# When an attention unit's output is normalised: the first unit earlier than the others

## The chip, the cores and the metric

The kernel runs on one core of a Trainium2 chip. The metric is the device time of one execution in microseconds, and the median of a few runs stands for a kernel. The core has five engines that work side by side, each through its own instructions in order: TensorE (PE in the profile, its weight loads PEld), VectorE (DVE), ScalarE (ACT), GpSimd (POOL) and SyncE (SP), which here issues nearly all DMA transfers.

## The reference

Four batches of eight-head attention over 576 positions with head dimension 64, whose scores carry a bias made by a tiny network from the distance of two positions; then a feed-forward layer with a rational activation over the 2304 tokens.

```
scores = q k^T / sqrt(64) + bias            # bias: relu(x w1 + b1) w2 per head, x from |i - j| and i
attn   = exp(scores - max) / (sum + 1e-9)
x      = attn v, heads side by side          # 2304 x 512
h      = x w_in                              # 2304 x 2048
g      = (a0 + a1 h + a2 h^2 + a3 h^3) / (1 + |b0||h| + |b1|h^2 + 1e-6)
out    = g w_out                             # 2304 x 512
```

## The kernel before

The program has three stages. The first makes the bias tables. The second, from about 45 to 270 us of the span, is attention; the third is the feed-forward layer, with each product as three float32r products of high and low halves.

Attention runs in *units*: unit u is one pair of heads of one batch, 16 in all (four pairs by four batches). A unit's 576 rows are cut into *steps* of 128 rows (the last 64 rows of two units share a step), 72 in all, and a *round* takes two steps. Round r forms the score products of steps 2r and 2r+1 (line 340), then, a round behind, transposes the probabilities of the two steps before (line 416), then multiplies transposed probabilities by V (line 485). DVE adds the bias and takes the row minimum of the negated scores (line 356), ACT takes the exponential (line 372) and copies the transposes out of PSUM (line 431). Each round DVE copies two products with V out of PSUM into the unit's tile `xs` (line 494). In the gaps of the rounds the layer's weights are split: POOL's copy `wm` (line 176), DVE's line 180, POOL's subtraction into `wil`/`wol` (line 187).

The sums of the exponentials are collected per unit; when a unit's last step is through, DVE adds 1e-9 and takes reciprocals, PE transposes them, DVE copies them to `rt`, and SP writes them to DRAM (`rs`, lines 455 and 460). `load_rb` (line 388) reads them back, broadcast over partitions, into `rb`. `e_norm` (line 400) multiplies `xs` by `rb` in place, on POOL for 14 of the 16 units, and puts a store of `xs` to DRAM (`xd`, line 402) on a list that the same round's end runs.

`done_to(k)` decides when: it is called at each round's end for the two steps that are complete; for unit u a step count `e` marks where the sums are ready (then `load_rb`), and a later count, the subject of the change, puts `e_norm` on the list `norms`. `rnd` takes at most one from this list in a round, into one of POOL's two places ("pool" ahead of DVE's score work, "pool2" after its first half) if the weight split has left that place empty. One round in three has both places taken.

Tiles come from pools that set when a buffer can be written again. `xs` has four buffers (`bufs=4`, line 490), so unit 4 writes into the buffer of unit 0, and its first write waits until unit 0's store has read it. `rb` has two, so unit 2's broadcast waits for unit 0's multiplication. SP issues in order; a transfer behind one that waits is not issued.

Of the kernel before, what the change touches and what calls it, by code (L numbers as in the profile page):

```python
# [37 lines left out]
def tile_attn_moe(  # L38
# [193 lines left out]
    with tc.manual_schedule():  # L232
# [3 lines left out]
        with ExitStack() as actx:  # L236
# [148 lines left out]
            def load_rb(u):  # L385
                t = rb[u] = npool.tile([P, S], F32, tag="rb", name=f"rb{u}")
                for j in range(2):
                    nc.sync.dma_start(  # L388
                        out=t[64 * j:64 * j + 64],
                        in_=rsum[u // 2][u % 2, j:j + 1, :].to_broadcast([64, S]),  # L390
                    )

            def e_norm(u):
                x = xs.pop(u)
                p, b = units[u]
                eng = V if u in (NX, NU - 1) else G
                f = rb.pop(u)

                def part(a, z):
                    op = eng.tensor_tensor(out=x[:, a:z], in0=x[:, a:z], in1=f[:, a:z], op=ALU.mult)  # L400
                    if z == S:
                        stores.append(lambda: nc.sync.dma_start(out=xd[b][:, p, :], in_=x))
                    return op

                return [lambda: part(0, S)]
# [95 lines left out]
            NS = len(steps)  # L501
            NU = len(units)
# [30 lines left out]
            def done_to(k):  # L533
                for u in range(NU - 1):
                    e = 2 * full[u]
                    if k == (e if u < NX else e - 2):
                        load_rb(u)
                    if u == NX:
                        if k == NS - 8:
                            x12.append(xs[u])  # L540
                            late.extend(e_norm(u))
                    elif k == (NS if u == NU - 2 else min(e + 4, NS - 3)):
                        norms.extend(e_norm(u))

            def run(todo):
# [43 lines left out]
            def rnd(r):  # L589
# [52 lines left out]
                if put:  # L642
                    put()
                run(stores)
                done_to(i - 2)
                done_to(i - 1)
                for x in plan["last"] + list(hi[1:]):
                    x()
# [11 lines left out]
            def finish():  # L660
                run(puts)
                mm1(0, 1)
                ZZ = (5, 7)
                main, ends, _, copy = e_tp(NS - 2, (2, 3), ZZ)
                weave(*(main[r] + ends[r] for r in range(2)))
                copy(1, 2)
                copy(0, 1)
                put_tails(NS - 2, 1, ZZ, ())
                recip(NS - 1)
                run(norms)  # L670
                run(stores)
                us = ended(NS - 1)
                main, ends, adds, copy = e_tp(NS - 1, (4, 6), ZZ, us)
                weave(*(main[r] + ends[r] + adds[r] for r in range(2)))
                copy(1, 2)
                copy(0, 1)
                put = [e_pv(NS - 3, 3), e_pv(NS - 2, 2)]
                put.pop(0)()
                put_tails(NS - 1, 1, ZZ, us)
                mm1(0, 0)  # L680
                put.pop(0)()
                put = e_pv(NS - 1, 6)
                done_to(NS)
                run(norms)
                run(stores)
                load_rb(NU - 1)
                load_x(1, 1, KD - 1, KD)
                put()

            with ExitStack() as bctx:  # L690
# [62 lines left out]
                for y, n in enumerate(order):  # L753
# [19 lines left out]
                    e = rpool.tile([P, EW], F32, tag="e", name=f"e{n}")  # L773
# [9 lines left out]
                    g, k = divmod(n, 8)  # L783
# [310 lines left out]
```

## Time and profile before

| | |
|---|---|
| median of 3 runs | 668.06 us (667.06 to 668.68) |
| profiled execution, own time | 667.56 us |
| its span, first to last instruction | 665.8 us |
| TensorE busy | 654.1 us, 98% of the span |
| VectorE busy | 561.6 us, 84% |
| ScalarE busy | 470.6 us, 71% |
| GpSimd busy | 153.5 us, 23% |
| mean granted TensorE clock | 0.995 |

Busy times are summed over an engine's instructions in the one profiled execution. Times on a row are microseconds from the span's start, and an idle time in brackets is what the engine waited before the instruction, with the event that ended it. Line numbers are those of the kernel.

### The profile page before, as it was taken

The page shows a single profiled execution, that of the slowest core. Times are in us where ns is not written, and L with a number is a line of the kernel's source. Part 1 is how long each engine was busy: PE and PEld are TensorE (multiplying, and loading weights), DVE is VectorE, ACT ScalarE, POOL GpSimd, SP SyncE. Part 2 cuts the span into 40 slices and gives each one's busy share as a digit, 9 for nine tenths or more (in the row PEclk, how much of TensorE's full clock was granted, in tenths as well). Part 3 has the DMA queues.
Part 4 walks back from the last instruction along what each step waited for, and adds up shares of the span by engine and source line. Part 5 has one row for each costly group of instructions (what it writes and reads, how often), then busy time and mean ns, then how long its engine had stood idle before and what let it go on. Part 6 is the DMA issues. An engine that isn't in the chain of part 4 may idle for free.

```text
span 665.8 us, 16141 instructions
## 1 busy us (share of the span) xinstructions
PE 654.1 (98%) x6276; PEld 550.0 (83%) x6276; DVE 561.6 (84%) x1102; ACT 470.6 (71%) x757; POOL 153.5 (23%) x108
## 2 busy tenths in 40 slices
PE   9999996999999999999999999999999999999997
PEld 6667885888888888988888888889988888888996
DVE  7997985888889996699998989979769779687776
ACT  7978996899999998677657466666655655455551
POOL 1000222334343340122122121222221221212211
PEclk9999998999999999999999999999999999999999
DMA  6898687688978974342744516768531301302031
GB/s 229 300 320 277 236 272 244 207 271 255 300 236 276 303 235 145 122 160 80 243 153 146 194 56 218 238 220 285 178 111 48 127 0 64 110 28 99 1 112 47
DMA packets 69901, 118.98 MB, mean 179 GB/s; under 512 B 9024, under 2 KB 30912, under 8 KB 69824
## 3 DMA queue, kind: packets, MB, share of 16 engines
q1 hardware_dynamic: 69680, 117.78, 53.6%
q8 instruction: 49, 0.80, 0.5%
q14 instruction: 28, 0.23, 0.1%
q10 hardware_dynamic: 144, 0.16, 0.1%
HBM read 79.17 MB, written 35.61 MB: 172 GB/s over the span
## 4 chain that ended last, share of the span: by engine, by line
PE 95%; ACT 2%; issue 1%; SPq 1%; DMA 1%; POOL 0%; DVE 0%; DVEq 0%; POOLq 0%
PE ps L313 30%; PE ps L922 30%; PE ps L485 12%; PE ps L340 11%; PE ps L769 6%; PE ps L416 6%; ACT p L372 1%; PE ps L720 1%; ACT pt L431 1%; DMA xd<-xs 1%; SPq L259 0%; POOL xs L400 0%; SPq L388 0%; DVE pre L943 0%; SPq L455 0%
## 5 line engine op out<-in xcount | busy, mean ns | idle before, releaser
L892 POOL TENSOR_TENSOR gl<-m,r 128x1024 fp32r<-128x1024 f32 (+1 forms) x39 | 85.6, 2194 | 299.5 <-DVE m L885 262.4
L843 ACT ACTIVATE w<-ps,babs 128x1024 f32<-128x1024 f32 (+1 forms) x40 | 41.2, 1031 | 107.8 <-PE ps L313 104.1
L372 ACT ACTIVATE p<-s,m 128x576 f32<-128x576 f32 x144 | 110.1, 781 | 0.6 <-DVE m L356 0.6
L356 DVE CUSTOM_DVE_ANT_0 s<-ps,bias 128x576 f32<-128x576 f32 (+1 forms) x144 | 95.2, 682 | 7.6 <-PE ps L340 3.3
L340 PE MATMUL ps<-qk 64*128 64x288 f32 (+1 forms) x640 | 82.8, 421 | 6.1 <-DVE xs L494 6.1
L431 ACT COPY pt<-ps 128x512 f32<-128x512 f32 (+1 forms) x109 | 71.8, 732 | 18.2 <-PE ps L416 18.2
L922 PE MATMUL ps<-wol,gh 128*128 128x512 f32 x216 | 84.2, 390 | 0.0
L922 PE MATMUL ps<-woh,gh 128*128 128x512 f32 x216 | 84.2, 390 | 0.0
L485 PE MATMUL ps<-pt,v 128*64 128x128 f32 (+1 forms) x1280 | 78.6, 266 | 0.8 <-ACT pt L431 0.5
L855 DVE SCALAR_TENSOR_TENSOR u<-w,babs,ps 128x1024 f32<-128x1024 f32 (+1 forms) x40 | 46.9, 1172 | 38.1 <-ACT t L844 38.0
L340 PEld LDWEIGHTS ps<-qk 64*128 64x128 f32 (+1 forms) x640 | 51.5, 177 | 26.0 <-DVE xs L494 7.5
L485 PEld LDWEIGHTS ps<-pt,v 128*64 128x64 f32 x1280 | 65.5, 137 | 5.7 <-ACT pt L431 1.6
L313 PE MATMUL ps<-xb,wih 128*128 128x512 f32 (+1 forms) x240 | 68.8, 367 | 0.0
L850 ACT ACTIVATE u<-u 128x1024 f32<-128x1024 f32 (+1 forms) x40 | 39.1, 977 | 40.2 <-DVE u L855 40.0
L416 PEld LDWEIGHTS ps<-ident,p 64*128 64x128 f32 x1296 | 51.1, 141 | 6.4 <-DVE m L356 0.6
L871 DVE SCALAR_TENSOR_TENSOR gh<-t,cst,r 128x1024 fp32r<-128x1024 f32 (+1 forms) x40 | 47.0, 1174 | 9.3 <-ACT r L852 6.9
L922 PE MATMUL ps<-woh,gl 128*128 128x512 f32 x216 | 53.8, 389 | 0.0
L416 PE MATMUL ps<-ident,p 64*128 64x64 f32 x1296 | 51.9, 228 | 0.1
L878 DVE SCALAR_TENSOR_TENSOR m<-u,qc,gh 128x1024 f32<-128x1024 f32 (+1 forms) x40 | 47.1, 1178 | 4.0
L313 PEld LDWEIGHTS ps<-xb,wih 128*128 128x128 f32 x240 | 44.5, 188 | 6.1
L885 DVE SCALAR_TENSOR_TENSOR m<-t,cst,m 128x1024 f32<-128x1024 f32 (+1 forms) x40 | 47.1, 1179 | 1.4
L864 DVE SCALAR_TENSOR_TENSOR t<-t,cst,ps 128x1024 f32<-128x1024 f32 (+1 forms) x40 | 47.0, 1175 | 1.4
(84 smaller groups left out, 1342.7 us busy)
## 6 DMA issues: line engine op xcount, KB each, us to landing
tab<-e SPq DMA_DIRECT2D x36, 295.5 KB
qk<-in_qkt_dram SPq DMA_DIRECT2D x16, 576.0 KB
wx<-in_w_in_dram SPq DMA_DIRECT2D x16, 512.0 KB
wx<-in_w_out_dram SPq DMA_DIRECT2D x16, 512.0 KB
v<-in_vp_dram SPq DMA_DIRECT2D x16, 320.0 KB
ws<-wh SPq DMA_DIRECT2D x20, 256.0 KB
ws<-wl SPq DMA_DIRECT2D x20, 256.0 KB
bias<-tab SPq DMA_DIRECT2D x16, 288.0 KB
```

Source lines behind the costliest of these rows:

```text
L313: on(T.matmul(hps[s][:, j, :w_], w[:, k, sl], x[:, k, :w_], start=(k == 0 and z == 0), stop=(k == KD - 1 and z == 2),), b + j)
L340: on(T.matmul(W[o, b, :SH], q[r, x], k[r, a * SH:(a + 1) * SH], start=True, stop=True), b)
L356: op = on(V.tensor_tensor_reduce(out=t3[:, a], in0=W[:, b:b + 2][:, a, :SH], in1=b3[:, a], scale=-0.125, scalar=least, op0=ALU.add, op1=AL ...
L372: A.activation(out=prob[i][:, z * S:z * S + S], in_=t, func=AF.Exp, bias=m, scale=-1.0, accum_out=sums[u % 4][:, k:k + 1],)
L416: on(T.transpose(W[:, b, o:o + 64], src[x, :], ident[x, x]), b)
L431: on(A.copy(out=t.rearrange("p x (r s) -> p r x s", r=2)[:, a:z], in_=W[:, to[a]:to[a] + z - a].rearrange("p r (x s) -> p r x s", s=64),), ...
L485: on(T.matmul(ps[y, o], vt[n][:, kc, y], w_, start=(kc == 0), stop=(kc == 4)), b, mem=(f"pt{i % 3}", f"tl{i // 2 % 2}"))
L864: on(V.scalar_tensor_tensor(out=rt[s, "t"], in0=rt[s, "t"], scalar=abs_[:, 1:2], in1=hp(s), op0=ALU.add, op1=ALU.mult,), *hb(s), mem="t")
L878: V.scalar_tensor_tensor(out=m, in0=rt[s, "u"], scalar=qc, in1=rt[s, "gh"].bitcast(F32), op0=ALU.add, op1=ALU.mult,)
L885: V.scalar_tensor_tensor(out=m, in0=rt[s, "t"], scalar=abs_[:, 0:1], in1=m, op0=ALU.add, op1=ALU.subtract)
L892: eng.tensor_tensor(out=lo, in0=rt[s, "m"], in1=rt[s, "r0"], op=ALU.mult)
L922: on(T.matmul(po[n, c], l[:, j, c * P:(c + 1) * P], r[fp][:, j, :], start=(first and x is a), stop=(last and x is z),), OB[c])
```

## The change

One number becomes an expression. For unit 0 the count that puts `e_norm` on the list is `e + 2`, for all others it stays `e + 4`.

```diff
@@ -539,7 +539,7 @@
                         if k == NS - 8:
                             x12.append(xs[u])
                             late.extend(e_norm(u))
-                    elif k == (NS if u == NU - 2 else min(e + 4, NS - 3)):
+                    elif k == (NS if u == NU - 2 else min(e + (4 if u else 2), NS - 3)):
                         norms.extend(e_norm(u))
```

For unit 0 `e` is 10. With `e + 4` the item goes on the list at the end of round 8; round 9 has no place, and round 10 takes it. With `e + 2` it goes on the list at the end of round 7, and round 8 has a place free. Unit 1's item, on the list from the end of round 9 in both kernels, finds round 10 free now, where before it went into round 11.

On POOL, in the rounds 7 to 11, the order before is this (a name's first number is the unit for `xs` and `rb`, the weight block for the others):

```order
L176 COPY wm1_0_1579<-wx1_0_1097 128x1024
L187 TENSOR_TENSOR wil0_897<-wm1_0_1579,wh1_0_1567 128x4x128
L176 COPY wm1_1_1816<-wx1_1_1099 128x1024
L187 TENSOR_TENSOR wol0_899<-wm1_1_1816,wh1_1_1692 128x512
L176 COPY wm2_0_1929<-wx2_0_1435 128x1024
L400 TENSOR_TENSOR xs0_990<-xs0_990,rb0_1554 128x576
L400 TENSOR_TENSOR xs1_1184<-xs1_1184,rb1_1677 128x576
L187 TENSOR_TENSOR wil1_901<-wm2_0_1929,wh2_0_1917 128x4x128
```

And in the changed kernel, on POOL in the same rounds:

```order
L176 COPY wm1_0_1579<-wx1_0_1097 128x1024
L400 TENSOR_TENSOR xs0_990<-xs0_990,rb0_1554 128x576
L187 TENSOR_TENSOR wil0_897<-wm1_0_1579,wh1_0_1567 128x4x128
L176 COPY wm1_1_1818<-wx1_1_1099 128x1024
L187 TENSOR_TENSOR wol0_899<-wm1_1_1818,wh1_1_1692 128x512
L176 COPY wm2_0_1931<-wx2_0_1435 128x1024
L400 TENSOR_TENSOR xs1_1184<-xs1_1184,rb1_1677 128x576
L187 TENSOR_TENSOR wil1_901<-wm2_0_1931,wh2_0_1919 128x4x128
```

Unit 0's multiplication has moved ahead of four weight instructions; unit 1's keeps its place in the sequence, but is tied to DVE's work of round 10, no longer of round 11.

On SP, from the end of round 8 to the end of round 10, the order before has unit 0's store of `xs` last:

```order
L460 DMA rs1_1765<-rt2_1764 2x2x64
L139 DMA wx3_0_1798<-in_w_in_dram 128x2048
L195 DMA woh0_898<-wh1_1_1692 128x512
L270 DMA v5_1801<-in_vp_dram 128x640
L264 DMA qk6_1803<-in_qkt_dram 128x1152
L388 DMA rb2_1905<-rs1_1765 64x576 x2
L139 DMA wx3_1_1908<-in_w_out_dram 128x2048
L259 DMA bias2_1910<-tab0_66 128x576
L259 DMA bias2_1910<-tab0_66 128x512
L259 DMA bias2_1910<-tab0_66 128x64
L455 DMA rs1_1765<-rt3_1990 2x4x128
L402 DMA xd0_71<-xs0_990 128x576
```

The changed kernel's SP has it in this place:

```order
L460 DMA rs1_1766<-rt2_1765 2x2x64
L402 DMA xd0_71<-xs0_990 128x576
L139 DMA wx3_0_1800<-in_w_in_dram 128x2048
L195 DMA woh0_898<-wh1_1_1692 128x512
L270 DMA v5_1803<-in_vp_dram 128x640
L264 DMA qk6_1805<-in_qkt_dram 128x1152
L388 DMA rb2_1907<-rs1_1766 64x576 x2
```

The store moves ahead of eleven issues, two weight loads (`wx`), the broadcast of unit 2 (`rb2`) and three bias loads among them.

Each of SP's issues also waits for one of eight DMA counters, DMAHW0 to DMAHW7, which the issues use in turn: an issue waits until the one eight places ahead has landed. For the broadcast of unit 0 this part of SP's order, the same in both kernels, is with its waits:

```order
L388 DMA rb0_1554<-rs0_1400 64x576 [waits DMAHW6_49]
L388 DMA rb0_1554<-rs0_1400 64x576 [waits DMAHW7_49]
L139 DMA wx2_1_1557<-in_w_out_dram 128x2048 [waits DMAHW0_49,Pool_49]
L259 DMA bias1_910<-tab3_69 128x576 [waits DMAHW1_49]
L259 DMA bias1_910<-tab3_69 128x512 [waits DMAHW2_49]
L259 DMA bias1_910<-tab3_69 128x64 [waits DMAHW3_49]
L264 DMA qk5_1562<-in_qkt_dram 128x1152 [waits DMAHW4_49,PE_49]
L388 DMA rb1_1677<-rs0_1400 64x576 [waits DMAHW5_49]
L388 DMA rb1_1677<-rs0_1400 64x576 [waits DMAHW6_49]
L195 DMA wih0_896<-wh1_0_1567 128x4x128 [waits DMAHW7_49,DVE_49]
```

Nothing moves here; the last row's issue waits for the second half of `rb0`, eight issues ahead of it.

## Rows read from the trace of the kernel before

**Rows 1.** The page, busy time of each engine.

```profile
PE 654.1 (98%) x6276; PEld 550.0 (83%) x6276; DVE 561.6 (84%) x1102; ACT 470.6 (71%) x757; POOL 153.5 (23%) x108
```

**Rows 2.** Chain of waits in order of time, 95 to 125 us: start, us, what.

```profile
104.75 1.42 POOL xs L400
...
106.19 0.47 SPq L388
...
111.01 3.60 DMA xd<-xs
...
115.08 2.29 PE ps L340 x8
```

**Rows 3.** Timeline of DVE: start, us, instruction, idle before it and releaser.

```profile
114.73 0.29 DVE L494 COPY xs<-ps 128x128 f32<-128x128 f32 x1 [6.99 <-DMA xd<-xs]
```

**Rows 4.** Timeline of PE, score products of round 11 and the next round's.

```profile
107.76 1.20 PE L340 MATMUL ps<-qk 64*64 64x288 f32 x16
115.08 2.29 PE L340 MATMUL ps<-qk 64*128 64x288 f32 x8 [6.12 <-DVE xs L494]
...
121.76 1.48 PE L340 MATMUL ps<-qk 64*128 64x288 f32 x10
```

**Rows 5.** Timeline of PE, first score products of rounds 6 and 7.

```profile
78.63 2.37 PE L340 MATMUL ps<-qk 64*64 64x288 f32 x24
...
84.51 1.73 PE L340 MATMUL ps<-qk 64*128 64x288 f32 x12
```

**Rows 6.** The same, first score products of rounds 15 and 16.

```profile
139.23 2.37 PE L340 MATMUL ps<-qk 64*64 64x288 f32 x24
...
145.11 2.21 PE L340 MATMUL ps<-qk 64*128 64x288 f32 x16
```

**Rows 7.** Engines by stretch: length, busy per engine (x instructions), PEclk, DMA share, GB/s.

```profile
98.00:100.00 2.00, 2.00 (x46) 1.74 (x44) 2.00 (x6) 1.22 (x5) 0.44 (x1) 1.00 0.11 27
108.00:115.00 7.00, 0.96 (x16) 0.31 (x8) 0.27 (x2) 1.80 (x6) 0.00 (x0) 0.85 0.95 291
115.00:121.00 6.00, 5.92 (x72) 5.14 (x74) 4.53 (x16) 3.46 (x6) 2.70 (x2) 0.61 0.51 147
121.00:660.00 539.00, 538.77 (x4320) 461.27 (x4317) 459.93 (x789) 370.01 (x560) 137.34 (x81) 1.00 0.49 160
```

**Rows 8.** Timeline of POOL, rounds 7 to 11.

```profile
85.44 1.04 POOL L176 COPY wm<-wx 128x1024 uint16<-128x1024 uint16 x1 [2.08 <-issue]
93.77 1.28 POOL L187 TENSOR_TENSOR wil<-wm,wh 128x512 fp32r<-128x512 f32 x1 [7.29 <-DVE wm L180]
96.81 1.04 POOL L176 COPY wm<-wx 128x1024 uint16<-128x1024 uint16 x1 [1.76 <-issue]
...
115.44 1.42 POOL L400 TENSOR_TENSOR xs<-xs,rb 128x576 f32<-128x576 f32 x1 [9.28 <-DVE wk L155]
```

**Rows 9.** Timeline of DVE, weight work of rounds 8, 9 and 11.

```profile
90.83 0.42 DVE L155 TENSOR_SCALAR wk<-wx 128x512 uint32<-128x512 uint32 x1
...
93.00 0.69 DVE L180 SCALAR_TENSOR_TENSOR wm<-wm,wh 128x512 uint32<-128x512 uint32 x1
...
98.79 0.69 DVE L180 SCALAR_TENSOR_TENSOR wm<-wm,wh 128x512 uint32<-128x512 uint32 x1
...
114.94 0.42 DVE L155 TENSOR_SCALAR wk<-wx 128x512 uint32<-128x512 uint32 x1
```

**Rows 10.** Timeline of SP's DMA issues, rounds 7 to 9.

```profile
84.64 1.13 SPq L388 DMA_DIRECT2D rb<-rs  x2
...
91.11 0.66 SPq L195 DMA_DIRECT2D wih<-wh  x1
...
98.60 0.26 SPq L460 DMA_DIRECT2D rs<-rt  x1
100.12 0.34 SPq L139 DMA_DIRECT2D wx<-in_w_in_dram  x1
...
101.18 0.54 SPq L270 DMA_DIRECT2D v<-in_vp_dram  x1
```

**Rows 11.** SP's issue and POOL's wait of one late unit.

```profile
252.12 1.11 SPq L388 DMA_DIRECT2D rb<-rs  x2
```

**Rows 12.** POOL's timeline for the same unit.

```profile
256.82 1.42 POOL L400 TENSOR_TENSOR xs<-xs,rb 128x576 f32<-128x576 f32 x1 [7.79 <-DMA rb<-rs]
```

## The prediction

> **What bounds the kernel now.** The page's busy times come first: TensorE is at work for 654.1 of 665.8 us [rows 1], so a change elsewhere counts only where TensorE stands still. Next, the chain of waits shows that the attention stage has one large hole. The chain leaves PE at about 101 us, runs through POOL's multiplication of unit 0, SP's queue and the store of `xs`, and comes back to PE at 115.08 [rows 2]. The timelines tell the same from both sides. DVE stood 6.99 us before its first copy into unit 4's `xs`, until the store of unit 0 had landed, since both units use one buffer [rows 3]; and PE stood 6.12 us in the middle of round 11's score products behind that copy [rows 4]. The stretches show what followed: the granted clock falls while PE stands (0.85 as the mean of 108 to 115 us), and from 115 to 121 us, with PE back at work, the mean is still 0.61, so that part of this stretch runs at 1.2 and not 2.4 GHz [rows 7]. From 121 to 660 us PE is busy for 538.77 of 539.00 us at clock 1.00 [rows 7]: nothing behind the hole would take back time gained there by already waiting for something else.
>
> **What the hole costs.** Not the 6.12 us alone, since the slow clock behind it belongs to it. I take whole rounds. Round 11 runs from 107.76 to round 12's first product at 121.76, 14.00 us [rows 4]. It has 24 score products, as every round with a shared 64-row step. Round 6, of the same shape, takes 84.51 - 78.63 = 5.88 us [rows 5], and round 15 takes 145.11 - 139.23 = 5.88 us [rows 6]. So the hole costs 14.00 - 5.88 = 8.12 us: 6.12 of standing still and 2.00 of slow clock. As a check, a mean of 0.61 over six microseconds is 0.39 x 6 = 2.3 us less of full clock, near 2.00.
>
> **The change part by part.** No instruction is added or removed, so busy times stay. Three things move.
>
> *Unit 0's multiplication*, one POOL instruction of 1.42 us [rows 8], goes from round 10 into round 8, ahead of the weight subtraction. It is tied to DVE's `wk` of that round, which ends at 90.83 + 0.42 = 91.25. In round 11 the same tie took 115.44 - (114.94 + 0.42) = 0.08 us [rows 8, 9], so it can start at 91.33 and end at 92.75. POOL has nothing to do between the end of a copy at 86.48 and 93.77 [rows 8], so the subtraction behind it is not moved: cost nothing, hidden in POOL's 7.29 us of waiting for DVE. It also needs `rb0`, and its arrival is not in the trace as a wait. Bounds: SP issued it from 84.64 on [rows 10]. From below, the nearest unit for which POOL stood waiting for its broadcast had it 256.82 - 252.12 = 4.70 us after the issue began [rows 11, 12], which would be 89.34 here. From above, the store of `wih0`, eight issues behind `rb0`'s second half on the same counter, was issued at 91.11 [rows 10], so `rb0` had landed by then. I take landed, no wait; the margin to 91.33 is at least 0.22 us.
>
> *Unit 0's store* is issued behind `rs` of the same round. SP was through with that at 98.60 + 0.26 = 98.86 but issued its next at 100.12 [rows 10]; that next one waited for an issue eight places ahead, and now the store stands in that place and waits for the same, so I take 100.12 and not 98.86. The multiplication is done by 92.75 and holds nothing up. Landing took 3.60 us from 111.01, with the DMA engines at 0.95 [rows 2, 7]; just ahead of 100 us they are at 0.11 [rows 7]. Taking the 3.60, the buffer is free at 103.72. DVE wants it at 114.73 - 6.99 = 107.74 [rows 3]. The slack is 4.0 us, and the whole wait goes. From below, with landing at once, nothing more is gained. The weight load that had the place at 100.12, and the four issues behind it, go back by one issue, about 0.4 us; the first of them that attention needs is unit 5's V, issued at 101.18 [rows 10] and used in round 12, more than 10 us later even in the faster kernel. Hidden.
>
> *Unit 2's broadcast* no longer waits on SP for unit 0's multiplication: it stood at the head of the queue until 106.19, right behind POOL's end at 106.17 [rows 2]. It and what stands behind it (a weight load and three bias loads) go out earlier; the stage's DMA work is the same. *Unit 1's multiplication* takes the place in round 10, one round earlier; its buffer is wanted two rounds later, in round 12. That is no gain and no loss.
>
> Sum: -8.12 us against the profiled execution's own 667.56, which is 1.76 us over its span: 659.44. The median of the runs shown is 668.06, 0.50 us higher, so the forecast for a median is **659.9 us**. In its favour I count nothing for the other parts.
>
> **A rule against it.** In round 8 DVE has one instruction with two inputs from SBUF beside the new POOL work, the line 180 at 93.00 [rows 9]; by the working above POOL ends 0.25 us ahead of it, so the two do not meet. The Trainium skill ("SBUF — State Buffer", section "SBUF: two separate sides") says that a GpSimd instruction and a DVE instruction with two SBUF inputs exclude each other for their whole length, the one that starts second waiting. The rows read here hold no such meeting, so they neither bear it out nor refute it.
>
> **Rivals.**
> 1. *The two engines meet.* If POOL starts a little later than 91.33 and DVE's line 180 had to wait for its end, the delay is at most the POOL instruction, 1.42 us [rows 8], in a round whose score work waits behind it: 8.12 - 1.42 = 6.70 gained, 661.4. For it: a margin of 0.25 us. Against it: weight subtractions on POOL, which also have two inputs, run beside DVE's score work in the same round, and PE shows no hole there. The skill's rule above would make it so.
> 2. *The store lands too late all the same.* Each microsecond past 107.74 comes off the gain, and the slow clock's 2.00 us come back if the hole is long. With three times 3.60 us it lands at 110.92, 3.2 us late: about 663, or 665 with all of the slow clock. Against it: 0.11 of DMA share as it starts.
> 3. *Another wait takes the hole's place*: some transfer that round 11 or 12 needs was landing during the 7 us in which DMA ran at 0.95 [rows 7], and nobody noticed. The candidate is unit 5's V; it would have to take over 15 us to matter. Then most of the 8.12 is given back: 667 to 668, no change.
> 4. *Slower: POOL stuck behind a late `rb0`.* POOL runs in order, and behind the multiplication stand the subtraction (1.28) and the copy (1.04) [rows 8] that DVE's line 180 at 98.79 [rows 9] waits for. With `rb0` at time T the copy ends at T + 1.42 + 1.28 + 1.04 + some 0.2 of gaps, so DVE and PE are late from T = 94.85 on, one for one. To eat the whole gain and 1.3 more, T would have to be about 104.3, some 20 us after the issue; T = 106 gives 11.15 of delay, 671.1. The issue at 91.11 speaks against it.
>
> **How the numbers follow.** The forecast has 0.82, with 659.0 to 661.2 as its own range: the three runs of before spread over 1.6 us, and a late `rb0` or queue may take some tenths. Rival 1 has 0.06, rival 2 0.05, rival 3 0.04, rival 4 0.03. For 8 in 10 and the unknowns on the slow side the range is 658.9 to 662.4, which takes in rival 1. This kernel's measurement can tell 0.2%, 1.3 us: faster is the forecast with rivals 1 and 2, 0.93; the same is rival 3, 0.04; slower is rival 4, 0.03.
>
> **What the next profile would show.** Right: DVE's copy into unit 4's `xs` with no wait on the store, round 11 at 5.9 us on PE, granted clock 1.00 from 100 to 121 us, POOL's line 400 at about 91.3, the store issued at about 100.1, every later stage 8.1 us earlier. Wrong: a PE hole anywhere between rounds 8 and 13, POOL's line 400 with a wait for `rb`, DVE's line 180 of round 8 behind an idle time, or, with the hole gone, a new wait after round 12 that PE did not have. A time over 663 would mean that one of these is there.

## The result, and the profile after

| | before | changed |
|---|---|---|
| median of 5 runs | 668.02 us (666.98 to 668.68) | 660.24 us (659.55 to 660.73) |
| ratio | | 0.9885, 95% interval 0.9870 to 0.9899 |
| span of the profiled execution | 665.8 us | 657.7 us |
| mean granted TensorE clock | 0.995 | 0.999 |

The kernel is 7.8 us faster; the forecast was 8.1 us less, 659.9. The spans of the two profiled executions differ by 8.1.

Round 11 on TensorE, which held the hole [rows 4], reads in the changed kernel's timeline of PE:

```profile
107.62 2.37 PE L340 MATMUL ps<-qk 64*64 64x288 f32 x24
109.82 1.28 PE L416 MATMUL ps<-ident,p 64*128 64x64 f32 x36
...
113.49 0.76 PE L340 MATMUL ps<-qk 64*128 64x288 f32 x4
```

All 24 score products stand in one row, and the round takes 113.49 - 107.62 = 5.87 us, where it took 14.00: 8.13 us gained in one round, the whole difference of the spans. DVE's first copy into unit 4's `xs`, which had waited 6.99 us for the store [rows 3], is the last row here (timeline of DVE):

```profile
106.92 0.68 DVE L167 SCALAR_TENSOR_TENSOR wh<-wx,wh 128x512 uint32<-128x512 uint32 x1
107.79 0.29 DVE L494 COPY xs<-ps 128x128 f32<-128x128 f32 x1 [0.19 <-issue]
```

It wants the buffer at the same time as before and has it. POOL's timeline answers to [rows 8]:

```profile
85.28 1.04 POOL L176 COPY wm<-wx 128x1024 uint16<-128x1024 uint16 x1 [2.08 <-issue]
91.19 1.42 POOL L400 TENSOR_TENSOR xs<-xs,rb 128x576 f32<-128x576 f32 x1 [4.87 <-DVE wk L155]
93.61 1.29 POOL L187 TENSOR_TENSOR wil<-wm,wh 128x512 fp32r<-128x512 f32 x1 [1.01 <-DVE wm L180]
96.66 1.04 POOL L176 COPY wm<-wx 128x1024 uint16<-128x1024 uint16 x1 [1.76 <-issue]
```

The multiplication sits in what was 7.29 us of waiting; the two instructions behind it come no later than before (93.61 for 93.77, 96.66 for 96.81, in an execution that runs 0.15 us ahead at this place). SP's timeline answers to [rows 10]:

```profile
97.39 0.26 SPq L460 DMA_DIRECT2D rs<-rt  x1
97.78 0.33 SPq L402 DMA_DIRECT2D xd<-xs  x1
98.16 0.43 SPq L139 DMA_DIRECT2D wx<-in_w_in_dram  x1
...
101.04 1.88 SPq L388 DMA_DIRECT2D rb<-rs  x2
102.97 0.58 SPq L139 DMA_DIRECT2D wx<-in_w_out_dram  x1
103.59 1.40 SPq L259 DMA_DIRECT2D bias<-tab  x3
```

The store goes out at 97.78, not at 111.01 [rows 2]; unit 2's broadcast at 101.04, not at 106.19. No engine waited for the store, but its landing can be told. The trace also records each DMA counter's steps, 16 for one transfer, and the last one is the landing: for the store of before it comes at 114.61, where the chain ends its 3.60 us [rows 2]. Here the last step comes at 100.31, 2.5 us after the issue and 7.5 us before DVE's copy. (The bias load at 103.59, eight issues behind, waits on the same counter.)

The stretches (columns as in [rows 7]) show no loss of clock and no new wait behind:

```profile
100.00:107.00 7.00, 7.00 (x122) 6.23 (x120) 6.18 (x26) 6.83 (x14) 3.14 (x3) 1.00 0.95 317
107.00:113.00 6.00, 5.95 (x108) 4.87 (x106) 5.59 (x19) 5.75 (x13) 1.28 (x1) 1.00 0.98 329
113.00:652.00 539.00, 538.70 (x4316) 461.18 (x4311) 459.45 (x788) 370.19 (x560) 137.37 (x81) 1.00 0.49 160
```

The DMA engines are at 0.95 and 0.98 here, as they were before while TensorE stood (0.95 from 108 to 115 us [rows 7]), and TensorE does not notice. From 113 to 652 us PE has 0.30 us of idle time; from 121 to 660 it had 0.23 before [rows 7].

### The profile page after: what moved, and what is told of

Same layout as the page of the kernel before. It is cut to its first block, busy times and chain, and to the rows that moved or that the text cites. A ratio compares the mean times of both kernels' runs of the same rounds, so it can differ in the third digit from the quotient of the medians.

```text
span 657.7 us, 16136 instructions
## 1 busy us (share of the span) xinstructions
PE 651.8 (99%) x6276; PEld 549.4 (84%) x6276; DVE 561.3 (85%) x1102; ACT 470.6 (72%) x757; POOL 153.6 (23%) x108
## 4 chain that ended last, share of the span: by engine, by line
PE 69%; ACT 1%; DVE 0%; issue 0%; DVEq 0%
PE ps L313 30%; PE ps L922 30%; PE ps L485 4%; PE ps L340 3%; PE ps L416 2%; ACT p L372 1%; ACT pt L431 0%; DVE pre L943 0%; ACT wh L164 0%; DVE s L356 0%; DVE wk L155 0%; DVE xs L494 0%; DVE m L356 0%; DVEq L356 0%
```

## The experiments

Three questions: is it the buffer of `xs` alone, and by which of two delays was its store late; how much of the hole is clock; and what margins does the new place have. All medians of "before" in these runs lie between 667.8 and 668.1 us.

**Unit 0's `xs` in a buffer of its own**, in the kernel before:

```diff
-    xs[x] = npool.tile([P, S], F32, tag="xs", name=f"xs{x}", bufs=4)
+    xs[x] = npool.tile([P, S], F32, tag="xs", name=f"xs{x}", bufs=4) if x else apool.tile([P, S], F32, tag="xs0", name="xs0")
```

> The kernel before, with a buffer of its own for unit 0's xs, so that unit 4 does not write into it; unit 0's multiplication stays in round 10 and its store in its old place. Theory (the hole of round 11 is DVE's wait for that buffer, and nothing else of the move counts): no hole, 668.0 - 7.8 = 660.2 us, though SP still stands until POOL's end at about 106.2. Rival (the gain comes from SP's queue, which the changed kernel no longer holds for unit 2's broadcast): SP's 3.8 us of standing stay and later transfers are late, over 664 us.

Measured 659.76 us (659.46 to 659.97), ratio 0.988 (0.9867 to 0.9894). The gain is there with nothing moved. SP, in its timeline, still stands for POOL and still stores at the old time:

```profile
106.18 1.11 SPq L388 DMA_DIRECT2D rb<-rs  x2
...
110.84 0.39 SPq L402 DMA_DIRECT2D xd<-xs  x1
```

and nothing on PE minds (timeline of PE, rounds 11 and 12):

```profile
107.75 2.37 PE L340 MATMUL ps<-qk 64*64 64x288 f32 x24
...
113.62 2.21 PE L340 MATMUL ps<-qk 64*128 64x288 f32 x16
```

So the wait for the buffer is the whole cost, and SP's standing as such costs nothing. The rival falls.

**Unit 0's `rb` in a buffer of its own**, in the kernel before. The multiplication and the store keep their places, but unit 2's broadcast is not held on SP:

```diff
-    t = rb[u] = npool.tile([P, S], F32, tag="rb", name=f"rb{u}")
+    t = rb[u] = npool.tile([P, S], F32, tag="rb", name=f"rb{u}") if u else apool.tile([P, S], F32, tag="rb0", name="rb0")
```

> The kernel before, with a buffer of its own for unit 0's rb, so that unit 2's broadcast no longer waits for unit 0's multiplication on SP; multiplication and store keep their places (round 10). Theory (two delays make the hole: the late place, and SP standing for the broadcast): the store follows the sums of round 10 (rt ready at 106.9) and is issued at about 107.7 in place of 111.0, lands 3.6 later at 111.3, DVE waits 3.5 in place of 7.0 us; 664.6 us, or 662.6 if the shorter hole leaves the clock at 1.00. Rival (only the place counts): 668. Rival (only SP's standing counts): 660.2.

Measured 664.46 us (664.32 to 665.52), ratio 0.9956 (0.9943 to 0.9970). The theory's first figure, 664.6, holds and neither rival does: part of the hole goes, part stays. The store is issued at 107.63 and landed at 111.75, half a microsecond later than I took. The timelines of DVE and PE:

```profile
111.87 0.29 DVE L494 COPY xs<-ps 128x128 f32<-128x128 f32 x1 [4.27 <-DMA xd<-xs]
```

```profile
107.61 1.20 PE L340 MATMUL ps<-qk 64*64 64x288 f32 x16
112.21 2.29 PE L340 MATMUL ps<-qk 64*128 64x288 f32 x8 [3.40 <-DVE xs L494]
118.37 1.00 PE L340 MATMUL ps<-qk 64*128 64x288 f32 x6
```

The hole is 3.40 us long, the round 10.76. So the late store of before had two causes: its place at the end of round 10, and SP standing for the multiplication ahead of a queue of loads, which put it 3.4 us later still (111.01 for 107.63).

**The early multiplication with the old place of the store**, in the changed kernel:

```diff
-    run(stores)
+    if r not in (8, 9):
+        run(stores)
```

> The changed kernel, with unit 0's store alone held back: issued at the end of round 10, its place before, while the multiplication stays in round 8 and the broadcast of unit 2 is not held. Theory: what counts is when the store is issued; the same as with the rb buffer of its own, issue at about 107.7, DVE waits some 3.5 us, 662.6 to 664.6 us. Rival (the early multiplication is what gains): 660.2.

Measured 665.63 us (664.52 to 666.26), ratio 0.9965 (0.9951 to 0.9979); one microsecond over the range I gave. The kind is right, the size is not: the store went out at 108.09, 0.4 later than I took, and DVE's copy started at 112.76, 4.7 us after the issue and not 3.6. DVE's copy, and the hole on PE:

```profile
112.76 0.29 DVE L494 COPY xs<-ps 128x128 f32<-128x128 f32 x1 [5.14 <-DMA xd<-xs]
```

```profile
107.64 1.20 PE L340 MATMUL ps<-qk 64*64 64x288 f32 x16
113.10 2.29 PE L340 MATMUL ps<-qk 64*128 64x288 f32 x8 [4.26 <-DVE xs L494]
119.83 1.00 PE L340 MATMUL ps<-qk 64*128 64x288 f32 x6
```

The early multiplication without the early store gives 2.2 us, by freeing SP of the same wait that the run with its own `rb` took away; the other 5.6 come only when the store is issued early as well. Two things tell this run from that one, and no run parts them: unit 1's store is issued right behind unit 0's (at 108.94), and the slow clock lasts longer. The five times fall in two groups, 664.52 and 664.60 us at a mean clock of 0.997, inside my range, and 665.63 to 666.26 at 0.995, where the profiled one is.

**The store at the end of round 9**, with `r not in (8,)` as the condition in the same place:

> The changed kernel, with unit 0's store held back by one round: issued at the end of round 9, behind unit 6's q and k. Theory (the store only has to land by 107.8, when DVE wants the buffer): issue at about 101, landing by 104.6 by the 3.6 us of before, no hole, 660.2 us. Rival (the store takes longer behind the q and k load, or the early place frees something else): a hole of 1 us or more, over 661.5 us.

Measured 660.09 us (659.28 to 662.50), ratio 0.9888 (0.9871 to 0.9906). By the time it is no different from the changed kernel, though one of the five executions took 662.50 (its trace is not on record). Its profile shows the edge (SP, DVE, then PE):

```profile
100.77 0.45 SPq L402 DMA_DIRECT2D xd<-xs  x1
```

```profile
108.90 0.29 DVE L494 COPY xs<-ps 128x128 f32<-128x128 f32 x1 [1.35 <-ACT p L372]
```

```profile
107.56 1.20 PE L340 MATMUL ps<-qk 64*64 64x288 f32 x16
109.24 1.24 PE L340 MATMUL ps<-qk 64*128 64x288 f32 x8 [0.48 <-DVE xs L494]
114.34 2.21 PE L340 MATMUL ps<-qk 64*128 64x288 f32 x16
```

The round takes 6.78 us, 0.9 more than without a hole. The store went out at 100.77, behind four transfers that the changed kernel has behind it: a weight load, a copy of a weight block (`woh`), unit 5's V and unit 6's q and k. The row names ACT as the releaser. I made a run of the same order with nothing to wait for, to tell whether that name is right.

**The same, and unit 0's `xs` in a buffer of its own** (both edits above together):

> The kernel with unit 0's store at the end of round 9, and a buffer of its own for unit 0's xs, so that nothing waits for this store. In the profile with the store in round 9, DVE's copy into unit 4's xs came 1.1 us late (108.90 for 107.79), and the profile names ACT's exponential as the releaser. Theory (it was the store, some 8 us on the way behind the load of q and k): the copy starts at its time, about 107.9, and round 11 takes 5.9 us again in place of 6.8. Rival (it was ACT, late for another reason): the copy at about 108.9 again, round 11 at 6.8 us. The medians, 660.1 here and there, can't tell these apart; the profile can.

Measured 659.92 us (659.63 to 660.00), ratio 0.9881 (0.9861 to 0.9902). In its timelines of SP, DVE and PE:

```profile
99.88 0.45 SPq L402 DMA_DIRECT2D xd<-xs  x1
```

```profile
107.72 0.29 DVE L494 COPY xs<-ps 128x128 f32<-128x128 f32 x1 [0.20 <-PE ps L485]
```

```profile
107.53 2.37 PE L340 MATMUL ps<-qk 64*64 64x288 f32 x24
113.41 2.21 PE L340 MATMUL ps<-qk 64*128 64x288 f32 x16
```

The copy starts at its time and round 11 takes 5.88 us, as the theory has it. But this run does not settle the question: in this execution SP was 0.9 us ahead, and by the store's counter it landed at 107.19, before the copy wanted the buffer, so the copy would have been on time with the shared buffer too.

The counter in the run with the shared buffer does settle it. There the store's last step comes at 108.78, and the copy starts at 108.90, 0.12 us behind it. It is the same 0.12 us in the three runs whose rows name the store: 114.61 to 114.73 in the kernel before, 111.75 to 111.87 with the `rb` of its own, 112.64 to 112.76 with the old place of the store. So it was the store, 8.0 us on its way (100.77 to 108.78), and not ACT.

**TensorE kept busy through the hole**, in the kernel before:

```diff
+    if r == 11:
+        for _ in range(25):
+            on(T.matmul(W[:, b, 0:P], ident, ident, start=True, stop=True), b)
     weave(sa[0] + sb[0], sa[1] + sb[1])
```

> The kernel before, with 25 throwaway products of the identity at the head of round 11 on PE, about 5.8 us at the full clock, written to a bank that the round's own products then overwrite: PE works through the hole instead of standing. The buffer wait is untouched. Theory (2.00 of the hole's 8.12 us are the slow clock behind it): the granted clock stays at 1.00 and 668.0 - 2.0 = 666.0 us. Rival (the 2.00 us are not the clock but work that starts late behind the wait): 668 or more.

Measured 666.25 us (665.80 to 666.94), ratio 0.9980 (0.9971 to 0.9989). The stretches and PE's timeline of this kernel:

```profile
108.00:115.00 7.00, 6.71 (x66) 5.91 (x65) 0.29 (x2) 1.78 (x6) 0.00 (x0) 1.00 0.99 310
115.00:121.00 6.00, 5.86 (x92) 4.95 (x94) 5.36 (x18) 4.54 (x9) 2.94 (x3) 1.00 0.40 134
```

```profile
107.73 5.85 PE L608 MATMUL ps<-ident 128*128 128x128 f32 x50
113.51 1.20 PE L340 MATMUL ps<-qk 64*64 64x288 f32 x16
115.06 1.24 PE L340 MATMUL ps<-qk 64*128 64x288 f32 x8 [0.34 <-DVE xs L494]
116.13 1.70 PE L416 MATMUL ps<-ident,p 64*128 64x64 f32 x36
...
120.15 2.21 PE L340 MATMUL ps<-qk 64*128 64x288 f32 x16
```

The last score products start at 115.06, as in [rows 4], so the buffer wait is untouched; the granted clock stays at 1.00 in both stretches, and the round ends 1.6 us sooner: 12.42 in place of 14.00. So 1.6 of the 2.00 us that I had put down to the clock are the clock. The other 0.4 I put down to work that starts late behind the wait: the transposes of this round, one row that takes 1.28 us in the changed kernel, take 1.70 here at the full clock.

**The multiplication one round earlier still** (`4 if u else 0`), in the changed kernel:

> The changed kernel with unit 0's multiplication one round earlier still (e in place of e + 2): in round 7's second place on POOL, right behind its broadcast's issue. POOL then waits for rb0, which shows when it lands: between 88.5 and 90.3 us by the forecast's bounds. Theory: POOL has nothing else until 93.6, so 660.2 us, no change to the changed kernel. Rival (POOL stuck behind a late rb0 delays the weight split): DVE's line 180 of round 8 or 9 late, over 661.5 us.

Measured 659.94 us (659.77 to 660.10), ratio 0.9881 (0.9866 to 0.9896). No change to the changed kernel, as forecast; the arrival of `rb0` was expected too early (88.5 to 90.3). The instructions of line 400 from 84 to 100 us, here and then in the changed kernel (88 to 93 us); POOLq is POOL's sequencer, the last two times of a row are its first and last start:

```profile
L400 POOLq EVENT_SEMAPHORE  x1: 43/43/43, 91.1 to 91.1; - x1
L400 POOL TENSOR_TENSOR xs<-xs,rb x1: 1417/1417/1417, 91.3 to 91.3; 128x576 f32<-128x576 f32 x1
```

```profile
L400 POOLq EVENT_SEMAPHORE  x1: 43/43/43, 90.0 to 90.0; - x1
L400 POOL TENSOR_TENSOR xs<-xs,rb x1: 1415/1415/1415, 91.2 to 91.2; 128x576 f32<-128x576 f32 x1
```

In the earlier place the instruction is tied to round 7's score work and not to round 8's `wk`, and yet it starts at 91.3, right behind its sequencer's wait; only `rb0` is left to wait for. (The timeline names `wk` as the releaser, which ends at 91.16 by coincidence.) The sequencer's times are the landing, and the counter agrees: the last step of `rb0`'s second half comes at 91.12 here and at 89.97 in the changed kernel, 6.6 and 5.5 us after the issue at 84.5, above the forecast's lower bound of 4.70. SP, with the store next in its queue, stood 2.7 us for POOL here, and that cost nothing either.

**The multiplication laid across DVE's line 180**, in the changed kernel; in round 8 it is tied to the first score instructions, which are issued ahead of it:

```diff
+    if r == 8:
+        op = e_ttr(i, 0, True)
     for x in plan["pool"]:
         ...
-    e_ttr(i, 0, True)
+    if r != 8:
+        e_ttr(i, 0, True)
     op = e_ttr(i, 1)
```

> The changed kernel with unit 0's multiplication tied to DVE's first score instructions of round 8 instead of its wk, so that it starts at about 92.3 and lies across DVE's line 180 at 92.85, both with two inputs from SBUF. Theory (the engines do not disturb each other here): line 180 starts at its time, 660.2 us. Rival (they exclude each other, as rival 1 of the forecast has it): line 180 starts only at POOL's end at about 93.7, the round 0.9 us late, 661.1 us.

Measured 660.31 us (660.04 to 660.70), ratio 0.9887 (0.9874 to 0.9901). The timelines of POOL and DVE of this kernel, then DVE of the changed one:

```profile
92.39 1.42 POOL L400 TENSOR_TENSOR xs<-xs,rb 128x576 f32<-128x576 f32 x1 [6.01 <-DVE m L356]
```

```profile
92.23 0.75 DVE L356 CUSTOM_DVE_ANT_0 s<-ps,bias 128x576 f32<-128x576 f32 x1
...
92.90 1.45 DVE L180 SCALAR_TENSOR_TENSOR wm<-wm,wh 128x512 uint32<-128x512 uint32 x1
```

```profile
92.85 0.69 DVE L180 SCALAR_TENSOR_TENSOR wm<-wm,wh 128x512 uint32<-128x512 uint32 x1
93.45 0.75 DVE L356 CUSTOM_DVE_ANT_0 s<-ps,bias 128x576 f32<-128x576 f32 x1
```

The engines do exclude each other: line 180 takes 1.45 us in place of 0.69. It shows as a longer instruction, not as idle time: POOL ends at 93.81, and line 180, started at 92.90, ends at 94.35. Meanwhile the score instruction at 92.23, with one input from PSUM, runs beside POOL at its usual 0.75. My theory was wrong and the rival right on the mechanism. The Trainium skill ("SBUF — State Buffer", section "SBUF: two separate sides") has the rule that of such a pair the one that starts first holds the shared port for its whole length and the other waits. This run agrees: POOL's end and 0.69 us make 94.50, and line 180 ended 0.15 us sooner. On PE the 0.76 us become 0.44: round 8 takes 96.53 - 90.28 = 6.25 us, in the changed kernel 96.03 - 90.22 = 5.81. The median shows nothing of that size.

**All units at `e + 2`**, in the changed kernel (`e + 2` in place of `e + (4 if u else 2)`):

> The changed kernel with all units' multiplications at e + 2, not only unit 0's. Theory (no other unit's buffer is waited for, since PE has no hole left between 113 and 652 us): 660.2 us. Rival (the earlier stores spread DMA work better, or POOL stands for broadcasts more often): 659 or less, or over 661.5 us.

Measured 659.90 us (659.73 to 660.26), ratio 0.9882 (0.9868 to 0.9895). The theory holds: from 113 to 652 us PE is busy for 538.34 of 539.00 us, in the changed kernel for 538.70, so no other unit's buffer held it up. The meeting of engines shows here too, this time with POOL as the one that waits: line 180 starts at 110.25 and keeps its 0.69 us, and the multiplication that starts beside it at 110.32 takes 1.90 in place of 1.42.

No version is faster than the changed kernel by more than these runs can tell. The five runs without a hole lie between 659.76 and 660.31 us.

## Why the prediction was right, point by point

*What bounds.* Right: one hole, nothing behind it takes the gain back. With the hole removed in two ways, by order and by a buffer of its own, the time is the same.

*The size, 8.12 us by whole rounds.* Right: 8.13 between the profiles, 7.8 between the medians, whose interval (0.9870 to 0.9899) is 6.7 to 8.7 us. To count 6.12 alone would have given 661.9. The split within the term was a little off: clock 1.6 and late work 0.4, by the run that kept TensorE busy, not 2.00 of clock. The check by the mean of 0.61 gave 2.3, too much.

*Unit 0's multiplication hidden on POOL.* Right: start 91.19 against a forecast 91.33. Both bounds on `rb0` held in the changed kernel: 89.97, between 89.34 and 91.11; with the multiplication in round 7 it was 91.12, at the upper edge. The lower bound was loose, since the late unit behind it read its broadcast when the DMA engines were less busy (0.46 from 248 to 268 us, 1.01 from 84 to 91). The margin to 91.33 was thin but hardly needed: the run that lays the multiplication across line 180 starts it 1.2 us later, at 92.39, and loses 0.44 us on PE in its profile and nothing that the median shows.

*The store.* Right in effect, by better luck than the working: it went out at 97.78 and not at 100.12, since the transfer eight ahead was through at 97.72 and not at 100.06 as in the profile before. The landing time of 3.60 us that I took was no bound: here it was 2.5, from two later issue places 4.1 and 4.6, and from behind the four transfers 8.0. Had it been 8.0 from the issue that I took, the store would have landed at 108.1, too late. What the changed kernel has in its favour is that its store goes ahead of those four.

*Two delays, one cure.* The forecast named both, the place and SP standing for the broadcast, and did not price them apart. The runs do: 3.3 us for SP's standing (667.79 to 664.46 with the broadcast freed), the other 4.5 of the 7.8 for the place.

*Rivals.* The meeting of engines is real (0.76 us on DVE, 0.44 on PE), and the forecast's 0.25 us that kept it away were a true margin: 0.24 in the changed kernel, from POOL's end at 92.61 to line 180 at 92.85. Its forecast price of 1.42 was an upper bound. A store that lands too late is real too, one round later. The other two showed nowhere.

## What to carry to other kernels

Where an engine waits for a buffer, follow the chain to the transfer that frees it, and look at what stands ahead of that transfer in its queue: here a queue held by another wait put the transfer 3.4 us later, and that was 3.3 of the 7.8 us. Price a hole on TensorE by whole rounds against undisturbed ones of the same shape, not by the idle time, since the slow clock behind it and the work that starts late belong to it. In these runs a store issued ahead of large loads landed in time, and the same store behind them once did not.

## What the runs showed of the hardware that was not expected

- The price of the slow clock did not follow the length of the hole. Rounds with holes of 3.40, 4.26 and 6.12 us lost 1.49, 2.06 and 2.01 us beyond the idle time (10.76, 12.19 and 14.00, less 5.87 and the hole); the round with 0.48, whose clock stayed at 1.00, lost 0.43. If 0.4 of each is late work, the clock's part is about 1.1, 1.7 and 1.6 us, an estimate from these rows.
- A 288 KB store took 2.5 us from issue to landing in the changed kernel, 3.4 to 4.6 in four runs that issue it at the end of round 10, and 7.3 and 8.0 behind four transfers of 1664 KB together (512, 256, 320 and 576).
- The last of a transfer's 16 counter steps can trail the others: for the store of 8.0 us the fifteenth came at 107.18 and the last at 108.78, for `rb0` in the run with the earlier multiplication at 90.07 and 91.12.
- Of a DVE instruction with two SBUF inputs and a GpSimd multiplication that meet, the one that starts second is stretched in its own row (DVE 0.69 to 1.45 us, GpSimd 1.42 to 1.90), so the meeting is found by comparing durations, not idle times.
- The releaser that a row names can be wrong where several are waited for: ACT in the run with the store in round 9, where the counter shows the DMA, and `wk` in the run with the earlier multiplication, where it shows `rb0`.
